# Attention and mixture-of-experts kernel: GpSimd issues only DMAs during the attention, and V tiles and expert weights go out in small portions

## The chip, the core and the metric

The kernel runs on one core of a Trainium2 chip. The metric is the device time of one execution in microseconds (us). "Before" is the kernel as it was, "the change" the edited one. A ratio is the mean time of one kernel's fast runs over that of the other's fast runs of the same rounds, so it is not quite the ratio of the medians quoted beside it. Below 1 is faster.

The engines are TensorE (PE; its weight loads PEld), VectorE (DVE), ScalarE (ACT), GpSimd (POOL) and SyncE (SP). In the traces GpSimd starts its instructions in the order of the program: the key copy at 66.57 us below starts only after a memset in front of it has waited 6.95 us. An instruction on GpSimd that waits holds up everything behind it on GpSimd, wanted or not.

## The reference, cut

```python
# attention: B=4, H=8, S=768, D=64; 8 global keys and a causal window of 96 keys
scores = scale * q @ k.T + bias;  a = softmax(where(is_global | is_local, scores, -1e9))
x = (a @ v)  ->  [3072, 512]
# top-1 mixture of 8 experts, with skipping
do = x @ w_skip > 0
e  = argmax(x @ w_gate);  g = softmax(x @ w_gate)[e]
out = x;  out[do] += g * (relu(x @ w1[e]) @ w2[e])      # w1, w2: 512x1024 and 1024x512 per expert
```

Inputs and outputs are fp32; the kernel's tiles are mostly bf16, cast by the DMAs.

## The kernel before

The attention works in 16 units: one head pair of one batch each, four units to a batch. Unit n's loop body computes the scores of unit n+2, transposes the q and k of unit n+4 and loads the q and k of unit n+8. Batch b can start its values only when the "global scores" of the batch are done; these need the first keys of all four of its head pairs, copied into the tile `kg`. After the attention, rows are gathered from DRAM by expert, go through the experts, and are scattered to the output.

```python
def load_v(b):                               # GpSimd, all of it
    vb = v_pool.tile([128, T, H, D1], BF16)
    for t in range(T):                       # T = 6
        nc.gpsimd.dma_start(out=vb[:, t, :, 0:D], in_=v_r[b, t])
    nc.gpsimd.memset(vb[:, :, :, D:D1], 1.0) # waits until the six loads have landed

def keys_global(n):                          # two small copies
    nc.gpsimd.tensor_copy(out=kg[...], in_=kts[n][...])

def load_vg(b):                              # a 128x512 product and a 128x8 copy
    nc.gpsimd.tensor_tensor(out=vg[:, b, :, 0:D], ...)
    nc.gpsimd.tensor_copy(out=vg[:, b, :, D], in_=head_m)

load_qk(0); load_qk(1); load_qk(2); load_qk(3); load_v(0)
for n in range(4):
    transposes(n, 1); transposes(n, 0); keys_global(n)
    ...                                      # scores of units 0 and 1
    load_qk(4 + n)
    if n == 1: load_vg(0)
load_v(1)
for b in range(1, B): load_vg(b)
for n in range(16):
    if hp == 0: global_scores(b)
    scores(n + 2, 0); values(n, 0); scores(n + 2, 1)
    transposes(n + 4, 1); keys_global(n + 4)
    ...; scores(n + 2, 2); values(n, 1); transposes(n + 4, 0)
    load_qk(n + 8)
    if n in (2, 5): load_v(2 if n == 2 else 3)
    if n == 8:                               # ten DMAs of 1 MB (as bf16)
        for e in range(5): load_weights(e, wearly)
    ...                                      # gating of batch b-1
# then 16 gathers, the weights of experts 5 to 7 among them, experts, 40 scatters: DMAs from GpSimd
```

In the built program every GpSimd DMA waits for the completion of the eighth GpSimd DMA before it: at most eight are in flight. The trace of the kernel before fits: its 12th, 13th and 14th GpSimd DMAs (9.77, 10.95 and 12.13 us) wait for a q, a k and a q load, which are the 4th, 5th and 6th. I call this the line of eight.

The softmax here doesn't subtract the row's maximum and nothing guards it: scores larger than these inputs give would overflow.

Of the kernel before, what the change touches and what calls it, by code (L numbers as in the profile page):

```python
# [9 lines left out]
BF16 = mybir.dt.bfloat16  # L10
I32 = mybir.dt.int32
AX = mybir.AxisListType
ALU = mybir.AluOpType
# [4 lines left out]
def kernel(  # L18
# [13 lines left out]
    nc = tc.nc  # L32
    B, H, S, D = q.shape
    NG = int(n_global)
    NL = int(n_local)
    T = S // 128
    N = B * S
    NT = N // 128
    DM = H * D
    HP = H // 2  # L40
    E, F = moe_w1.shape[0], moe_w1.shape[2]
    DC = DM // 128
    FC = F // 128
# [7 lines left out]
    D1 = D + 1  # L51
    KG = 128 // H
    NV = 5
    RSPACE = 4096
    EARLY = 5
# [5 lines left out]
    wearly = ctx.enter_context(tc.tile_pool(name="wearly", bufs=1))  # L61
# [4 lines left out]
    acon = attn.enter_context(tc.tile_pool(name="acon", bufs=1))  # L66
# [9 lines left out]
    v_r = v.rearrange("b h (t p) d -> b t p h d", p=128)  # L76
    w1_r = moe_w1.rearrange("e (c p) f -> e p c f", p=128)
    w2_r = moe_w2.rearrange("e (c p j) d -> e p c (j d)", p=128, j=2)

    units = [(b, hp) for b in range(B) for hp in range(HP)]  # L80
    raws, qts, kts, g_sbs, a_sbs, vbs = {}, {}, {}, {}, {}, {}

    def load_qk(n):
        b, hp = units[n]
        qr = raw_pool.tile([P, 2, R * D], BF16, tag="qr", name="qr")
        kr = raw_pool.tile([P, 2, R * D], BF16, tag="kr", name="kr")
        nc.gpsimd.dma_start(out=kr[:, :, :], in_=k_r[b, :, 2 * hp:2 * hp + 2, :])
        nc.gpsimd.dma_start(out=qr[:, :, :], in_=q_r[b, :, 2 * hp:2 * hp + 2, :])
        raws[n] = (qr, kr)

    def load_v(b, ones=True):
        vb = v_pool.tile([128, T, H, D1], BF16, tag="vb", name="vb")
        for t in range(T):
            nc.gpsimd.dma_start(out=vb[:, t, :, 0:D], in_=v_r[b, t])  # L94
        nc.gpsimd.memset(vb[:, :, :, D:D1], 1.0)
        vbs[b] = vb

    w1_sb, w2_sb = {}, {}

    def load_weights(e, pool):  # L100
        w1_sb[e] = pool.tile([128, DC, F], BF16, name=f"w1_{e}")
        w2_sb[e] = pool.tile([128, FC // 2, 2 * DM], BF16, name=f"w2_{e}")
        nc.gpsimd.dma_start(out=w1_sb[e][:, :, :], in_=w1_r[e])
        nc.gpsimd.dma_start(out=w2_sb[e][:, :, :], in_=w2_r[e])

    manual = tc.manual_schedule()
    manual.__enter__()
# [2 lines left out]
    nc.gpsimd.iota(row128_i[:, :], pattern=[[1, 128]], base=0, channel_multiplier=0)  # L110
    part_i = setup.tile([128, 1], I32)
    nc.gpsimd.iota(part_i[:, :], pattern=[[0, 1]], base=0, channel_multiplier=1)
    load_qk(0)
    load_qk(1)
    load_qk(2)
    load_qk(3)
    load_v(0)
    colid_i = setup.tile([128, NCOL], I32)
    nc.gpsimd.iota(colid_i[:, :], pattern=[[RSPACE // 128, E], [1, CAP // 128]], base=0,
                   channel_multiplier=0)  # L120
# [9 lines left out]
    for h in range(H):  # L130
        nc.sync.dma_start(out=vg_f[h * KG:(h + 1) * KG, :, :],
                          in_=v[:, h, 0:KG, :].rearrange("b k d -> k b d"))
    wg_f = acon.tile([128, DC, E + 1], FP32)
    for dc in range(DC):
# [3 lines left out]
    part_f = setup.tile([128, 1], FP32)  # L138
# [3 lines left out]
                            scalar2=None, op0=ALU.is_equal)  # L142
    kg = []
    for s in range(2):
# [6 lines left out]
                            scalar2=None, op0=ALU.subtract)  # L151
    nc.vector.tensor_scalar(out=rel[:, 128:W], in0=row128_i[:, 0:NL], scalar1=part_f[:, 0:1],
                            scalar2=128.0, op0=ALU.subtract, op1=ALU.add)
    far = acon.tile([128, W], FP32)
    for bound, op in ((0.0, ALU.is_lt), (float(NL), ALU.is_ge)):
        nc.vector.tensor_scalar(out=far[:, :], in0=rel[:, :], scalar1=bound, scalar2=1.0e6,
                                op0=op, op1=ALU.mult)
        nc.vector.tensor_tensor(out=rel[:, :], in0=rel[:, :], in1=far[:, :], op=ALU.add)
    mask8 = acon.tile([128, H, 2, W], BF16)
    for h in range(H):  # L160
        nc.scalar.activation(out=mask8[:, h, :, :],
                             in_=rel[:, :].unsqueeze(1).to_broadcast([128, 2, W]),
# [5 lines left out]
                                   op=ALU.arith_shift_right)  # L168
    gkey_i = acon.tile([128, 1], I32)
    nc.vector.tensor_single_scalar(out=gkey_i[:, :], in_=part_i[:, :], scalar=KG - 1,  # L170
                                   op=ALU.bitwise_and)
# [6 lines left out]
    head_m = acon.tile([128, H], FP32)  # L178
    nc.vector.tensor_scalar(out=head_m[:, :], in0=row128_i[:, 0:H], scalar1=ghead[:, 0:1],
                            scalar2=None, op0=ALU.is_equal)  # L180
    gconst = acon.tile([128, H], FP32)
    for h in range(H):
# [5 lines left out]
                            op0=ALU.mult)  # L188
    grel = acon.tile([128, 128], FP32)
    nc.vector.tensor_scalar(out=grel[:, :], in0=row128_i[:, :], scalar1=gk[:, 0:1], scalar2=None,  # L190
                            op0=ALU.subtract)
# [2 lines left out]
    nc.vector.tensor_single_scalar(out=grel[:, :], in_=grel[:, :], scalar=float(NL), op=ALU.is_ge)  # L194
    m0g = acon.tile([128, 128], BF16)
    nc.vector.tensor_tensor(out=m0g[:, :], in0=gw1[:, :], in1=grel[:, :], op=ALU.add)
    vg = acon.tile([128, B, H, D1], BF16)

    def load_vg(b):
        nc.gpsimd.tensor_tensor(  # L200
            out=vg[:, b, :, 0:D],
            in0=vg_f[:, b, :].unsqueeze(1).to_broadcast([128, H, D]),
            in1=head_m[:, :].unsqueeze(2).to_broadcast([128, H, D]), op=ALU.mult)
        nc.gpsimd.tensor_copy(out=vg[:, b, :, D], in_=head_m[:, :])

    ones_bf = setup.tile([128, 128], BF16)
    nc.vector.memset(ones_bf[:, :], 1.0)
# [2 lines left out]
                            op0=ALU.is_ge)  # L210
# [10 lines left out]
    def late_constants():  # L221
        nc.vector.tensor_copy(out=wg[:, :, :], in_=wg_f[:, :, :])
        nc.vector.tensor_copy(out=eorder[:, :], in_=eorder_i[:, 0, :])
        nc.vector.tensor_copy(out=run[:, :], in_=eorder_i[:, 1, :])
        nc.vector.tensor_copy(out=val_k[:, :, 1], in_=tt_i[:, :])
        nc.vector.tensor_copy(out=val_k[:, :, 0], in_=part_f[:, 0:1].to_broadcast([128, NT]))
        nc.vector.memset(slots[:, :, :], 0.0)
# [3 lines left out]
    def transposes(n, which):  # L231
        b, hp = units[n]
        raw = raws[n][which]
        ps = ps_ms.tile([128, R, P], BF16, tag="ms", name="tr")
        for r in range(R):
            for hh in range(2):
                nc.tensor.transpose(out=ps[hh * D:(hh + 1) * D, r, :],
                                    in_=raw[:, hh, r * D:(r + 1) * D], identity=ident[0:P, 0:P])
        if which == 0:
            qt = t_pool.tile([128, R, P], BF16, tag="qt", name="qt")  # L240
            nc.vector.tensor_copy(out=qt[:, :, :].bitcast(I32), in_=ps[:, :, :].bitcast(I32))  # L241
            qts[n] = qt
        else:
            kt = t_pool.tile([128, S], BF16, tag="kt", name="kt")
            nc.scalar.activation(out=kt[:, :].rearrange("a (p r) -> a p r", r=R),  # L245
                                 in_=ps[:, :, :].rearrange("a r p -> a p r"),
                                 func=ACT.Copy)
            kts[n] = kt

    def keys_global(n):  # L250
        b, hp = units[n]
        for hh in range(2):
            h = 2 * hp + hh
            nc.gpsimd.tensor_copy(out=kg[b % 2][hh * D:(hh + 1) * D, hp, h * KG:(h + 1) * KG],  # L254
                                  in_=kts[n][hh * D:(hh + 1) * D, 0:KG])

    def global_scores(b):
        g_sb = att_pool.tile([128, S], BF16, tag="g_sb", name="g_sb")
# [83 lines left out]
    def x_out(b):  # L342
        nc.sync.dma_start(
            out=x_dram[b * S:(b + 1) * S, :].rearrange("(t p) d -> p t d", p=128),
            in_=xbs[b][:, :, :])
# [116 lines left out]



    for n in range(4):
        transposes(n, 1)
        transposes(n, 0)
        keys_global(n)
        if n < 2:
            for g in range(3):  # L470
                scores(n, g)
        load_qk(4 + n)
        if n == 1:
            load_vg(0)
    late_constants()
    load_v(1)
    for b in range(1, B):
        load_vg(b)
    for n in range(NU):
        b, hp = units[n]  # L480
        if hp == 0:
            global_scores(b)
        m, j = n + 4, n + 2
        if j < NU:
            scores(j, 0)
        values(n, 0)
        if j < NU:
            scores(j, 1)
        if m < NU:
            transposes(m, 1)  # L490
            keys_global(m)
        if b > 0 and hp < 3:
            logits(b - 1, hp)
        if j < NU:
            scores(j, 2)
        values(n, 1)
        if m < NU:
            transposes(m, 0)
        if m + 4 < NU:
            load_qk(m + 4)  # L500
        if n in (2, 5):
            load_v(2 if n == 2 else 3)
        if n == 8:
            for e in range(EARLY):
                load_weights(e, wearly)
        if hp == HP - 1:
            x_out(b)
        if b > 0 and hp == 2:
            gate(b - 1)
        if b > 0 and hp == 3:  # L510
            gate_rest(b - 1)
            place((b - 1) * T, T, colid_i, gat_pool, ps_ms, "ms")
# [9 lines left out]
    wlate = ctx.enter_context(tc.tile_pool(name="wlate", bufs=1, reuse_waits="tile"))  # L522
# [76 lines left out]
    def experts(group, first):  # L599
        rows, src, gate_ = slot_rows()  # L600
        for e in range(E):
            gather(e, src)
            if first and e % 2 == 1 and EARLY + e // 2 < E:
                load_weights(EARLY + e // 2, wlate)
        xt = expert_in(0)
        for e in range(E):
            nxt = expert_in(e + 1) if e + 1 < E else None
            expert(e, xt, rows, gate_, group)
            if first:
                for t in range(3 * e, 3 * e + 3):  # L610
                    skip_out(t, group)
            xt = nxt

    experts("first", True)
    manual.__exit__(None, None, None)

# [5 lines left out]
                                   op=ALU.bitwise_and)  # L622
# [5 lines left out]
                                   op=ALU.arith_shift_right)  # L628
# [3 lines left out]
    with tc.For_i(1, n_rounds, 1):  # L632
        nc.vector.tensor_single_scalar(out=colid[:, :], in_=colid[:, :], scalar=CAP // 128,
                                       op=ALU.add)
# [38 lines left out]
```

## Time and profile before

| what | value |
|---|---|
| median time | 260.75 us (3 runs, 259.92 to 261.82) |
| profiled span | 260.2 us (of a run of 262.22 us) |
| global scores of batch 0 / 1 / 2 / 3 done | 30.7 / 68.8 / 97.9 / 126.6 us |
| last attention output done, first gather | 141.3, 157.2 us |
| last scatter issued | 248.8 us |

The page's slices show the span in 40 parts of 6.5 us; a digit is the busy share in tenths, PEclk the granted TensorE clock in tenths.

```profile
PE   1561698200696849854972511799992599994000
...
PEclk9999999655599558965797755589999599999655
DMA  5993991599449992999999998999999344434420
```

TensorE is nearly empty in the fourth slice and in slices 8 to 10 (46 to 65 us). The GpSimd timeline says why. Its columns are start, duration, engine, line, operation, output<-input, shape, count, and in brackets the idle time before it with what ended that.

```profile
12.13 0.87 POOL L94 DMA_DIRECT2D vb<-in_v_dram  x1 [0.31 <-DMA qr<-in_q_dram]
21.41 0.31 POOL L95 MEMSET vb<- 128x48 bf16 x1 [8.40 <-DMA vb<-in_v_dram]
...
30.00 5.29 POOL L94 DMA_DIRECT2D vb<-in_v_dram  x6
42.01 0.32 POOL L95 MEMSET vb<- 128x48 bf16 x1 [6.71 <-DMA vb<-in_v_dram]
...
57.43 1.82 POOL L94 DMA_DIRECT2D vb<-in_v_dram  x2 [1.68 <-DMA kr<-in_k_dram]
66.20 0.31 POOL L95 MEMSET vb<- 128x48 bf16 x1 [6.95 <-DMA vb<-in_v_dram]
66.57 0.44 POOL L254 COPY kg<-kt 64x16 bf16<-64x16 bf16 x2
```

Three of the four memsets stand 6.7 to 8.4 us behind V loads. The key copy at 66.57 comes right after the third one, although it had nothing to do with V. The list of waits adds up who paid (total us, number of times, longest):

```profile
POOL vb L95 <- DMA vb<-in_v_dram: 26.9, 4, 8.4
...
PE gp L262 <- POOL kg L254: 29.9, 8, 15.5
...
PE tr L237 <- DMA kr<-in_k_dram: 4.9, 1, 4.9
```

GpSimd's own waits were 26.9 us; TensorE's wait for the key copies behind them was 29.9 us. A table of stages, cut at the times above, gives for each stretch its length, then busy us and instruction count of PE, PEld, DVE, ACT and POOL, the mean granted clock, the DMA share (in this view it can exceed 1) and GB/s:

```profile
30.70:68.80 38.10, 17.15 (x298) 11.48 (x298) 14.89 (x33) 13.84 (x22) 21.77 (x36) 0.73 1.20 108
68.80:97.90 29.10, 22.01 (x360) 15.97 (x361) 19.47 (x59) 17.07 (x26) 12.24 (x23) 0.73 1.01 120
97.90:126.60 28.70, 21.25 (x359) 15.52 (x361) 19.45 (x59) 17.01 (x26) 8.94 (x18) 0.74 0.90 166
126.60:141.30 14.70, 9.73 (x192) 7.93 (x191) 11.50 (x40) 8.37 (x13) 0.00 (x0) 0.96 1.12 225
141.30:157.20 15.90, 4.80 (x67) 4.18 (x67) 9.37 (x42) 2.29 (x3) 0.00 (x0) 0.61 1.11 227
157.20:260.20 103.00, 65.24 (x449) 43.59 (x449) 17.69 (x29) 19.03 (x32) 60.58 (x62) 0.81 0.64 149
```

The first row is batch 0 until the global scores of batch 1: 38.1 us for 17 us of TensorE work. The next two are batches 1 and 2. The fifth ends with the gather rows ready; the sixth is the experts.

### The profile page before, as it was taken

Reading aid. Unit: us, or ns where it says so; the run is one execution under the profiler, and the core shown is the slowest. Engines: PE = TensorE matmul, PEld = TensorE weight load, DVE = VectorE, ACT = ScalarE, POOL = GpSimd, SP = SyncE. Lnnn points to the kernel's source line nnn. Section 1 sums busy time; section 2 is a strip of 40 time slices with the busy share of each in tenths; the row PEclk is TensorE's granted clock in tenths of the full one; section 3 lists DMA queues with packets and bytes.
Section 4 is the critical chain, followed back from the end, with each engine's and each line's share of the span. In section 5 each row is a group of like instructions: output and inputs, shape, how many; then the busy total and the mean of one; then the engine's idle time right before and its main releaser. Section 6 shows DMA issues by size and latency. Waiting matters only on the chain.

```text
span 260.2 us, 4730 instructions
## 1 busy us (share of the span) xinstructions
PE 152.4 (59%) x1877; PEld 106.7 (41%) x1877; DVE 104.2 (40%) x311; ACT 91.1 (35%) x144; POOL 123.5 (47%) x183
## 2 busy tenths in 40 slices
PE   1561698200696849854972511799992599994000
PEld 1450376000375627643662500557770277762000
DVE  7440079400268764887389380212200432323000
ACT  5860389000396508933670300023330033330000
POOL 8806945971348323611000006836261777777730
PEclk9999999655599558965797755589999599999655
DMA  5993991599449992999999998999999344434420
GB/s 84 177 127 55 154 153 8 104 202 117 62 66 138 51 216 29 199 202 210 229 229 211 229 231 179 161 238 223 226 202 244 118 133 148 136 99 117 118 52 1
DMA packets 50520, 38.24 MB, mean 147 GB/s; under 512 B 30276, under 2 KB 39492, under 8 KB 50496
## 3 DMA queue, kind: packets, MB, share of 16 engines
q0 software_dynamic: 45568, 34.62, 84.6%
q1 hardware_dynamic: 4928, 3.30, 4.9%
q8 instruction: 16, 0.26, 0.4%
q14 instruction: 8, 0.07, 0.1%
HBM read 54.68 MB, written 13.63 MB: 263 GB/s over the span
## 4 chain that ended last, share of the span: by engine, by line
DMA 35%; PE 21%; POOL 14%; DVE 10%; ACT 8%; issue 7%; POOLq 0%; ACTq 0%; DVEq 0%
DMA vb<-in_v_dram 9%; PE yps L586 7%; DMA x_rows<-xb 6%; PE hps L579 5%; DMA xg<-x_rows,src 5%; DMA w<-in_moe_w_dram 5%; DMA out_dram<-y,rows 5%; DMA kr<-in_k_dram 3%; DMA qr<-in_q_dram 3%; ACT a L287 3%; PE gp L262 3%; ACT a L295 2%; DVE xb L332 2%; POOL xg L547 2%; ACT xts L362 2%
## 5 line engine op out<-in xcount | busy, mean ns | idle before, releaser
L582 ACT ACTIVATE ht<-hps 128x512 bf16<-128x512 f32 x32 | 19.0, 597 | 66.0 <-PE hps L579 66.0
L547 POOL DMA_INDIRECT xg<-x_rows,src x16 | 15.7, 980 | 51.7 <-DMA x_rows<-xb 38.1
L301 DVE TENSOR_TENSOR a<-a,mask 128x896 bf16<-128x896 bf16 (+1 forms) x48 | 29.2, 612 | 22.3 <-ACT a L287 12.1
L586 PE MATMUL yps<-w,ht 128*128 128x512 bf16 x128 | 30.8, 394 | 7.9 <-DVE y L591 7.9
L591 DVE SCALAR_TENSOR_TENSOR y<-yps,gate,xg 128x512 f32<-128x512 f32 x16 | 11.9, 750 | 55.4 <-PE yps L586 28.5
L287 ACT ACTIVATE a<-sc 128x896 bf16<-128x896 f32 x32 | 28.9, 923 | 9.0 <-PE sc L282 8.2
L579 PE MATMUL hps<-xt,w 128*128 128x256 bf16 x256 | 31.8, 287 | 0.0
L556 POOL DMA_INDIRECT out_dram<-xb,skip_k x24 | 24.1, 1004 | 13.6 <-DMA w<-in_moe_w_dram 6.8
L262 PE MATMUL gp<-qt,kg 128*128 128x384 bf16 x32 | 11.9, 513 | 29.9 <-POOL kg L254 29.9
L579 PEld LDWEIGHTS <-w 128*128 128x128 bf16 x256 | 26.1, 103 | 4.2
L94 POOL DMA_DIRECT2D vb<-in_v_dram x24 | 21.2, 904 | 2.7 <-DMA kr<-in_k_dram 2.0
L586 PEld LDWEIGHTS <-ht 128*128 128x128 bf16 x128 | 12.8, 100 | 22.5 <-issue 9.9
L265 ACT ACTIVATE g_sb<-gp,gbias 128x384 bf16<-128x384 f32 x8 | 4.6, 581 | 48.1 <-PE gp L262 48.1
L282 PE MATMUL sc<-qt,kt 64*128 64x224 bf16 x192 | 19.8, 296 | 2.8 <-DVE qt L241 1.3
L319 PE MATMUL av<-vb,a 128*128 128x65 bf16 x192 | 19.1, 207 | 0.0
L262 PEld LDWEIGHTS <-kg 128*128 128x128 bf16 x32 | 4.0, 135 | 35.5 <-POOL kg L254 32.4
L332 DVE TENSOR_TENSOR xb<-av,rc 128x384 bf16<-128x384 f32 x32 | 17.8, 558 | 1.1
L326 PE MATMUL av<-vb,a 128*96 128x65 bf16 x160 | 18.3, 219 | 0.0
L594 POOL DMA_INDIRECT out_dram<-y,rows x16 | 15.9, 995 | 4.9 <-issue 3.7
L319 PEld LDWEIGHTS <-a 128*128 128x128 bf16 x192 | 17.0, 117 | 0.0
L326 PEld LDWEIGHTS <-a 128*96 128x96 bf16 x160 | 15.6, 138 | 0.0
L254 POOL COPY kg<-kt 64x16 bf16<-64x16 bf16 x32 | 6.7, 210 | 17.6 <-ACT kt L245 16.4
(115 smaller groups left out, 246.6 us busy)
## 6 DMA issues: line engine op xcount, KB each, us to landing
w<-in_moe_w_dram POOLq DMA_DIRECT2D x16, 1024.0 KB, 22.4
kr<-in_k_dram POOLq DMA_DIRECT2D x16, 192.0 KB, 5.2
qr<-in_q_dram POOLq DMA_DIRECT2D x16, 192.0 KB, 5.4
vb<-in_v_dram POOLq DMA_DIRECT2D x24, 128.0 KB, 6.7
x_rows<-xb SPq DMA_DIRECT2D x4, 768.0 KB, 11.4
out_dram<-xb,skip_k POOLq DMA_INDIRECT x24, 2.6
xg<-x_rows,src POOLq DMA_INDIRECT x16, 12.6
out_dram<-y,rows POOLq DMA_INDIRECT x16, 2.7
```

Source lines behind the costliest of these rows:

```text
L94: nc.gpsimd.dma_start(out=vb[:, t, :, 0:D], in_=v_r[b, t])
L262: nc.tensor.matmul(out=gp[:, :, :], lhsT=kg[b % 2][:, hp, :], rhs=qts[b * HP + hp][:, :, u * (P // 2):(u + 1) * (P // 2)], start=(hp == 0) ...
L282: nc.tensor.matmul(out=sc[:, hh, kk, 0:R * wp].rearrange("a (r p) -> a r p", r=R), lhsT=kt[rows, t * 128:(t + 1) * 128], rhs=qt[rows, :, t ...
L287: nc.scalar.activation(out=a[:, :, :].rearrange("a h (k p r) -> a h k p r", k=2, r=R), in_=sc[:, :, :, 0:W].rearrange("a h k (r p) -> a h ...
L301: nc.vector.tensor_tensor(out=a[:, :, 0:wid], in0=a[:, :, 0:wid], in1=m[:, :, 0:wid], op=ALU.mult)
L319: nc.tensor.matmul(out=av[:, jj, hh, :], lhsT=a_sbs[n, t // 2][:, hh, (t % 2) * W:(t % 2) * W + 128], rhs=vb[:, t, h, :], start=False, sto ...
L326: nc.tensor.matmul(out=av[0:NL, jj, hh, :], lhsT=a_sbs[n, p // 2][:, hh, c:c + NL], rhs=vb[:, p, h, :], start=False, stop=(jj == 2 and hh ...
L332: nc.vector.tensor_tensor(out=xb[:, 3 * u:3 * u + 3, 2 * hp * D:(2 * hp + 2) * D].rearrange("p j (h d) -> p j h d", h=2), in0=av[:, :, :, ...
L547: nc.gpsimd.indirect_dma_start(out=xg[e][:, c, :], out_offset=None, in_=x_dram[:, :], in_offset=bass.IndirectOffsetOnAxis(ap=src[:, 2 * e ...
L556: put(nc.gpsimd.indirect_dma_start(out=out[:, :], out_offset=bass.IndirectOffsetOnAxis(ap=skip_k[:, t:t + 1], axis=0), in_=xbs[t // T][:, ...
L579: nc.tensor.matmul(out=hps[:, j, :], lhsT=w1_sb[e][:, dc, c2 * 256 + j:(c2 + 1) * 256:2], rhs=xt[:, dc, :], start=(dc == 0), stop=(dc == D ...
L586: nc.tensor.matmul(out=yps[:, :], lhsT=ht[:, f // 2, f % 2, c * 128:(c + 1) * 128], rhs=w2_sb[e][:, f // 2, (f % 2) * DM:(f % 2 + 1) * DM] ...
```

## The change: its intent, and the diff

GpSimd is to hold nothing but DMA issues during the attention, so that no wait of a load stands before work that computes. The memset, key copies and vg products go to VectorE. V tiles go out three per unit and the early weight halves one per unit from unit 1 on, so that the DMA queues are filled evenly.

```diff
-    def load_v(b, ones=True):
+    def make_v(b):
         vb = v_pool.tile([128, T, H, D1], BF16, tag="vb", name="vb")
-        for t in range(T):
-            nc.gpsimd.dma_start(out=vb[:, t, :, 0:D], in_=v_r[b, t])
-        nc.gpsimd.memset(vb[:, :, :, D:D1], 1.0)
+        nc.vector.memset(vb[:, :, :, D:D1], 1.0)
         vbs[b] = vb
+    def load_v(b, t):
+        nc.gpsimd.dma_start(out=vbs[b][:, t, :, 0:D], in_=v_r[b, t])
...  load_vg: both instructions from nc.gpsimd to nc.vector
...  keys_global: two nc.gpsimd.tensor_copy become one nc.vector product with a 0/1 mask of the halves
...  start: load_v(0, 0), load_v(0, 1) before load_qk(2), load_v(0, 2) before load_qk(3)
+    extra = [V tiles of batches 1, 2, 3 in order]
+    halves = {1: 1, 2: 1, 3: 1, 4: 1, 5: 1, 6: 1, 7: 1, 8: 1, 9: 1, 10: 1}
...  in the loop over units:
         if m + 4 < NU:
             load_qk(m + 4)
-        if n in (2, 5):
-            load_v(2 if n == 2 else 3)
-        if n == 8:
-            for e in range(EARLY):
-                load_weights(e, wearly)
+        if n in (0, 2, 4):
+            make_v(1 + n // 2)
+            load_vg(1 + n // 2)
+        for kind in range(3):
+            if extra:
+                _, vb_, t = extra.pop(0)
+                load_v(vb_, t)
+        for _ in range(halves.get(n, 0)):
+            load_half(wq.pop(0), wearly)
```

More of the change, by code (lines that the diff above doesn't have):

```diff
@@ L89, in load_qk, with load_half @@
         raws[n] = (qr, kr)
-    def load_v(b, ones=True):
+    def make_v(b):
         vb = v_pool.tile([128, T, H, D1], BF16, tag="vb", name="vb")
-        for t in range(T):
-            nc.gpsimd.dma_start(out=vb[:, t, :, 0:D], in_=v_r[b, t])
-        nc.gpsimd.memset(vb[:, :, :, D:D1], 1.0)
+        nc.vector.memset(vb[:, :, :, D:D1], 1.0)
         vbs[b] = vb
+    def load_v(b, t):
+        nc.gpsimd.dma_start(out=vbs[b][:, t, :, 0:D], in_=v_r[b, t])
     w1_sb, w2_sb = {}, {}
-    def load_weights(e, pool):
-        w1_sb[e] = pool.tile([128, DC, F], BF16, name=f"w1_{e}")
-        w2_sb[e] = pool.tile([128, FC // 2, 2 * DM], BF16, name=f"w2_{e}")
-        nc.gpsimd.dma_start(out=w1_sb[e][:, :, :], in_=w1_r[e])
-        nc.gpsimd.dma_start(out=w2_sb[e][:, :, :], in_=w2_r[e])
+    def load_half(i, pool):
+        e = i // 2
+        if i % 2 == 0:
+            w1_sb[e] = pool.tile([128, DC, F], BF16, name=f"w1_{e}")
+            nc.gpsimd.dma_start(out=w1_sb[e][:, :, :], in_=w1_r[e])
+        else:
+            w2_sb[e] = pool.tile([128, FC // 2, 2 * DM], BF16, name=f"w2_{e}")
+            nc.gpsimd.dma_start(out=w2_sb[e][:, :, :], in_=w2_r[e])
     manual = tc.manual_schedule()
@@ L112 @@
     nc.gpsimd.iota(part_i[:, :], pattern=[[0, 1]], base=0, channel_multiplier=1)
+    make_v(0)
     load_qk(0)
     load_qk(1)
+    load_v(0, 0)
+    load_v(0, 1)
     load_qk(2)
+    load_v(0, 2)
     load_qk(3)
-    load_v(0)
+    for t in range(3, T):
+        load_v(0, t)
     colid_i = setup.tile([128, NCOL], I32)
@@ L196 @@
     nc.vector.tensor_tensor(out=m0g[:, :], in0=gw1[:, :], in1=grel[:, :], op=ALU.add)
+    half_m = acon.tile([128, 2], BF16)
+    nc.vector.tensor_scalar(out=half_m[:, 1:2], in0=part_f[:, :], scalar1=float(D), scalar2=None,
+                            op0=ALU.is_ge)
+    nc.vector.tensor_scalar(out=half_m[:, 0:1], in0=part_f[:, :], scalar1=float(D), scalar2=None,
+                            op0=ALU.is_lt)
     vg = acon.tile([128, B, H, D1], BF16)
     def load_vg(b):
-        nc.gpsimd.tensor_tensor(
+        nc.vector.tensor_tensor(
             out=vg[:, b, :, 0:D],
@@ L203, in load_vg @@
             in1=head_m[:, :].unsqueeze(2).to_broadcast([128, H, D]), op=ALU.mult)
-        nc.gpsimd.tensor_copy(out=vg[:, b, :, D], in_=head_m[:, :])
+        nc.vector.tensor_copy(out=vg[:, b, :, D], in_=head_m[:, :])
     ones_bf = setup.tile([128, 128], BF16)
@@ L251, in keys_global @@
         b, hp = units[n]
-        for hh in range(2):
-            h = 2 * hp + hh
-            nc.gpsimd.tensor_copy(out=kg[b % 2][hh * D:(hh + 1) * D, hp, h * KG:(h + 1) * KG],
-                                  in_=kts[n][hh * D:(hh + 1) * D, 0:KG])
+        nc.vector.tensor_tensor(
+            out=kg[b % 2][:, hp, 2 * hp * KG:2 * (hp + 1) * KG].rearrange("p (h k) -> p h k", h=2),
+            in0=kts[n][:, 0:KG].unsqueeze(1).to_broadcast([128, 2, KG]),
+            in1=half_m[:, :].unsqueeze(2).to_broadcast([128, 2, KG]), op=ALU.mult)
     def global_scores(b):
@@ L461, in place @@
         nc.vector.tensor_tensor(out=slots[:, :, :], in0=slots[:, :, :], in1=sp[:, :, :], op=ALU.add)
+    extra = [("v", 1, t) for t in range(T)]
+    wq = list(range(2 * EARLY))
+    for b in (2, 3):
+        extra += [("v", b, t) for t in range(T)]
+    halves = {1: 1, 2: 1, 3: 1, 4: 1, 5: 1, 6: 1, 7: 1, 8: 1, 9: 1, 10: 1}
     for n in range(4):
@@ L472 @@
         load_qk(4 + n)
-        if n == 1:
-            load_vg(0)
+    load_vg(0)
     late_constants()
-    load_v(1)
-    for b in range(1, B):
-        load_vg(b)
     for n in range(NU):
@@ L603, in experts @@
             if first and e % 2 == 1 and EARLY + e // 2 < E:
-                load_weights(EARLY + e // 2, wlate)
+                load_half(2 * (EARLY + e // 2), wlate)
+                load_half(2 * (EARLY + e // 2) + 1, wlate)
         xt = expert_in(0)
```

## The prediction

> **What bounds the kernel now.** By the chain of waits and the GpSimd timeline, three stretches.
>
> 1. Start, 12 to 30.6 us. GpSimd issues the last V tile at 12.1 us, then sits 8.4 us before the ones-memset of that V buffer, until its DMAs land (21.4). The global-key copies queue behind it on the in-order engine; the global scores are only complete at 30.6, although the last transposes ended at 18.4.
> 2. Attention, 31 to 141 us. Batch 0's four units take 14 us. GpSimd repeats the pattern: memset waiting 6.7 us (35 to 42), 4.5 us of vg products, issues, then memset waiting 7 us more (59 to 66). TensorE is idle in 51.6 to 67.1 (15.5 us charged to the global-key copy) and, but for three matmuls, from 45. Batches 1 and 2 take 28 us each, batch 3 some 17, limited by the VectorE/ScalarE/TensorE chain (each 60 to 75% busy).
> 3. 141 to 260 us. Gathers start at 157.2. The x_rows write (15 us, shared with the late early-weight traffic) ends the wait, but VectorE delivers the gather rows only at 155.9, so the write hides about 1 us. Then gathers, 6.3 MB of late weights and 40 scatters at 1.3 us each: GpSimd issue and DMA bound, 103 us.
>
> **What the change does.** No GpSimd instruction in the attention waits for a V transfer in front of compute work. VectorE gets 16 key products (about 0.2 us), 4 vg products (estimate 0.7 us, from the 128x384 product's 0.56) with casts, 4 memsets: 6 us in all, perhaps 4 on the path, as VectorE is nearly limiting. GpSimd's elementwise work no longer overlaps VectorE: during the vg products the mask product took 1.45 us instead of 0.62. The Trainium skill (GPSIMD Engine Reference, Specifications) says the two share SBUF interfaces when VectorE has two SBUF inputs; this trace agrees.
>
> **Size.**
> - Start: the loop begins near 21.5 instead of 30.6: -9 us.
> - Batch 0 to 1: global scores of batch 1 finish near 40 instead of 68.8; of this -9 is the start, so -20 net of about 2.5 us of VectorE work.
> - Rest of attention: +2 us of VectorE work.
> - Given back: the DMA queue. Measured rates: V 155 GB/s, q/k about 175, weights 213. One unit's q/k+V+weight half is 2.25+2.55+4.9 = 9.7 us (estimate) against 7 us of compute. q/k loads fall behind near units 9 to 11 and stall transposes: +4 us (0 to 10).
> - x_rows no longer shares with weights: -0.7 only, since the row computation ends at the same time.
> - Gathers to end: unchanged, 103 us. Early weights land near 115 instead of 153, but nothing waits for them.
>
> Attention ends near 118 instead of 141.3. Predicted time: 237 us, range 226 to 248. Chances: faster 0.96, same 0.03, slower 0.01.
>
> **What would show it.** GpSimd timeline: no memset, no copies, only DMA issues until the first gather, which comes near 133. TensorE's 15.5 us gap before the global scores gone; those of batch 0 done near 21.5, of batch 1 near 40. A TensorE wait for k/q DMAs of a few us in batch 2 or at its end would confirm the give-back. Weight landings within 50 to 120. Time from last attention output to first gather still about 15 us, first gather to end still about 103.
>
> **What would make it wrong.** Only eight GpSimd DMAs are in flight; weight halves in that line could delay q/k or V far more than 4 us (towards 250). Denser TensorE work may be granted a lower clock (it alternates 1.0 and 0.5 now), lengthening batches and experts. If the final stage was itself slowed by the weight backlog, 225 is possible.

## More of the kernel before

The gap in `vb` that the memset fills lies between the bytes that the DMAs write, so the dependency tracking takes the two as overlapping and orders them as written (this is read from the program; the trace shows the wait).

For k tiles TensorE waited once, at the very first load.

## The result, and the profile after

The change ran in 243.35 us (median of 4 runs, 242.59 to 243.99) against 260.34 us before; ratio 0.938, 95% interval 0.930 to 0.946. Executions over 1.5% slower than the fastest of the same kernel are left out of the means. Of the four runs before, 261.82 us is 1.7% above the fastest, which counts as slow. The profiled span fell from 260.2 to 242.2 us (runs of 262.22 and 243.99 us).

The slices of the change, now 6.05 us each:

```profile
PE   1579895995494847768544038699943999992000
...
PEclk9999998897569575559857556999995799998555
DMA  5999999999999999999630039999994355343310
```

The holes in TensorE's row in the first third are gone, and the DMA row is full until 115 us; TensorE has new thin slices, the 4s at 73 to 79 and 85 to 91 us (slices 13 and 15). Slice 11 is a 4 too, but there it waits 3.41 us for VectorE's gating work, as it also did before (up to 4.2 us). The same table of stages as before:

```profile
21.50:40.70 19.20, 15.27 (x299) 11.21 (x300) 15.57 (x43) 13.87 (x22) 13.92 (x18) 1.00 1.38 161
40.70:69.80 29.10, 22.09 (x359) 16.07 (x361) 21.06 (x67) 17.16 (x26) 12.15 (x17) 0.73 1.39 212
69.80:108.10 38.30, 25.43 (x359) 18.55 (x361) 20.35 (x63) 17.33 (x26) 8.31 (x12) 0.63 1.29 208
108.10:123.20 15.10, 11.13 (x191) 9.13 (x191) 11.51 (x40) 8.53 (x13) 0.00 (x0) 0.84 0.76 156
123.20:138.80 15.60, 4.97 (x67) 4.35 (x67) 9.45 (x43) 2.29 (x3) 0.00 (x0) 0.61 0.15 52
138.80:242.20 103.40, 65.10 (x449) 43.40 (x449) 17.93 (x29) 19.10 (x32) 60.55 (x62) 0.80 0.61 143
```

| stage | before | change | difference |
|---|---|---|---|
| start to global scores of batch 0 | 30.7 | 21.5 | -9.2 |
| batch 0, to global scores of batch 1 | 38.1 | 19.2 | -18.9 |
| batch 1 | 29.1 | 29.1 | 0.0 |
| batch 2 | 28.7 | 38.3 | +9.6 |
| batch 3 | 14.7 | 15.1 | +0.4 |
| last output to first gather | 15.9 | 15.6 | -0.3 |
| gathers, experts, end | 103.0 | 103.4 | +0.4 |
| sum | 260.2 | 242.2 | -18.0 |

In the list of waits, the one for key copies on GpSimd is gone, a short one for VectorE is left, and the one for k has grown:

```profile
PE tr L251 <- DMA kr<-in_k_dram: 13.3, 4, 5.1
...
PE gp L276 <- DVE qt L255: 2.9, 1, 2.9
```

GpSimd still waits for other engines: the three V loads at 28.18 us waited 3.97 us for VectorE to write the ones of their buffer, and the q load at 46.09 us waited 4.46 us for a transpose on TensorE.

Of the 28 us won in front, batch 2 gives a third back. TensorE's timeline shows where: it waits for a k tile in two of the batch's transposes.

```profile
79.73 0.85 PE L251 MATMUL tr<-ident,kr 96*64 96x96 bf16 x16 [4.26 <-DMA kr<-in_k_dram]
...
89.22 0.85 PE L251 MATMUL tr<-ident,kr 96*64 96x96 bf16 x16 [3.53 <-DMA kr<-in_k_dram]
```

The GpSimd timeline shows the lateness. These lines are from units 5 and 6:

```profile
61.67 0.78 POOL L108 DMA_DIRECT2D w<-in_moe_w_dram  x1
62.66 0.65 POOL L87 DMA_DIRECT2D kr<-in_k_dram  x1 [0.21 <-PE av L340]
67.13 0.64 POOL L88 DMA_DIRECT2D qr<-in_q_dram  x1 [3.83 <-DMA w<-in_moe_w_dram]
...
73.43 0.75 POOL L105 DMA_DIRECT2D w<-in_moe_w_dram  x1 [0.19 <-issue]
74.64 0.65 POOL L87 DMA_DIRECT2D kr<-in_k_dram  x1 [0.46 <-PE sc L296]
79.28 0.64 POOL L88 DMA_DIRECT2D qr<-in_q_dram  x1 [3.99 <-DMA w<-in_moe_w_dram]
```

The k tile issued at 62.66 is the one that TensorE starts on at 79.73, 17 us later. The q issues behind the k issues wait 3.8 to 4.0 us each for a weight half: the line of eight is full. The Trainium skill (DMA: Bandwidth & Descriptors, section "Two DMAs through the same engine are not ordered") says that within one queue of one DMA engine descriptors start in order. That a small load behind a large one therefore waits for it is my inference, and this trace agrees: the weight half issued at 61.67 is the eighth DMA before the q issue of 79.28, which its landing released, and the k tile issued 1 us after that half landed at 79.7. Over all k tiles the median time from issue to landing rose from 5.2 to 7.8 us, the longest from 8.3 to 17.0 us.

### The profile page after: what moved, and what is told of

Its sections match the earlier page's. It is cut to its first block, busy times and chain, and to the rows that moved or that the text cites. A ratio compares the mean times of both kernels' runs of the same rounds, so it can differ in the third digit from the quotient of the medians.

```text
span 242.2 us, 4714 instructions
## 1 busy us (share of the span) xinstructions
PE 155.8 (64%) x1877; PEld 110.8 (46%) x1877; DVE 109.1 (45%) x341; ACT 91.8 (38%) x144; POOL 111.0 (46%) x139
## 5 line engine op out<-in xcount | busy, mean ns | idle before, releaser
L315 DVE TENSOR_TENSOR a<-a,mask 128x896 bf16<-128x896 bf16 (+1 forms) x48 | 28.2, 588 | 21.8 <-ACT a L301 11.7
L599 PE MATMUL hps<-xt,w 128*128 128x256 bf16 x256 | 31.2, 283 | 0.0
L97 POOL DMA_DIRECT2D vb<-in_v_dram x24 | 21.5, 906 | 11.3 <-DMA vb<-in_v_dram 4.0
L333 PE MATMUL av<-vb,a 128*128 128x65 bf16 x192 | 20.7, 215 | 0.0
L251 PE MATMUL tr<-ident,kr 96*64 96x96 bf16 x256 | 11.4, 251 | 13.3 <-DMA kr<-in_k_dram 13.3
L340 PE MATMUL av<-vb,a 128*96 128x65 bf16 x160 | 19.7, 229 | 0.0
L88 POOL DMA_DIRECT2D qr<-in_q_dram x16 | 10.4, 650 | 19.2 <-DMA w<-in_moe_w_dram 11.7
L333 PEld LDWEIGHTS <-a 128*128 128x128 bf16 x192 | 18.6, 125 | 0.0
L614 POOL DMA_INDIRECT out_dram<-y,rows x16 | 15.9, 994 | 4.9 <-issue 3.7
L340 PEld LDWEIGHTS <-a 128*96 128x96 bf16 x160 | 17.1, 147 | 0.0
L251 PEld LDWEIGHTS <-kr 96*64 96x64 bf16 x256 | 8.8, 140 | 17.1 <-DMA kr<-in_k_dram 14.0
L259 ACT ACTIVATE kt<-tr 128x768 bf16<-128x768 bf16 x16 | 13.0, 810 | 8.5 <-PE tr L251 8.5
```

The costliest lines, as they stand in the source:

```text
L97: nc.gpsimd.dma_start(out=vbs[b][:, t, :, 0:D], in_=v_r[b, t])
L251: nc.tensor.transpose(out=ps[hh * D:(hh + 1) * D, r, :], in_=raw[:, hh, r * D:(r + 1) * D], identity=ident[0:P, 0:P])
L315: nc.vector.tensor_tensor(out=a[:, :, 0:wid], in0=a[:, :, 0:wid], in1=m[:, :, 0:wid], op=ALU.mult)
L333: nc.tensor.matmul(out=av[:, jj, hh, :], lhsT=a_sbs[n, t // 2][:, hh, (t % 2) * W:(t % 2) * W + 128], rhs=vb[:, t, h, :], start=False, sto ...
L340: nc.tensor.matmul(out=av[0:NL, jj, hh, :], lhsT=a_sbs[n, p // 2][:, hh, c:c + NL], rhs=vb[:, p, h, :], start=False, stop=(jj == 2 and hh ...
L599: nc.tensor.matmul(out=hps[:, j, :], lhsT=w1_sb[e][:, dc, c2 * 256 + j:(c2 + 1) * 256:2], rhs=xt[:, dc, :], start=(dc == 0), stop=(dc == D ...
```

## The experiments

Theory Q: the early weight halves, placed in the line ahead of q and k, cost batch 2 its 9.6 us. Theory V, its rival: the work added to VectorE, or a lower granted clock (0.63 in batch 2 against 0.74), lengthened it. A second pair concerns the gain. Theory M: nearly all of it is the memset no longer waiting. Theory E: the elementwise work had to leave GpSimd. Every run gave the reference's result, within its tolerance. Call 1 (first four runs) and call 3 (last four) had the kernel before at 260.79 and 260.17 us. Call 2 fell on a chip where it took 270.46 us, so its runs are compared by ratio.

### Weights back at unit 8

```diff
-    halves = {1: 1, 2: 1, 3: 1, 4: 1, 5: 1, 6: 1, 7: 1, 8: 1, 9: 1, 10: 1}
+    halves = {8: 10}
```

> The changed kernel with one part undone: all ten early weight halves issued at head pair 8, as before the change. Theory Q (the weight halves stand in the DMA line ahead of the q/k loads and cost batch 2 its 9.3 us): the two k waits of 4.3 and 3.5 us vanish, batch 2 takes 26 to 27 us again instead of 35.6, time 233 to 236 us. Theory V (batch 2 is longer because of VectorE's added work or a lower granted clock): batch 2 stays near 35 us, time 242 to 244 us. Both: gathers to end unchanged at 103 us, as long as the weights land before the gathers.

Measured: 234.73 us, ratio 0.901 (0.897 to 0.905). The waits of TensorE for k, and the batch 2 row of its stage table:

```profile
PE tr L251 <- DMA kr<-in_k_dram: 5.2, 1, 5.2
```

```profile
69.40:98.30 28.90, 21.45 (x360) 15.65 (x361) 20.07 (x63) 17.01 (x26) 1.49 (x2) 0.74 1.12 221
```

The one wait left is the very first load of the kernel. Batch 2 takes 28.9 us with 20.1 us of VectorE work, against 28.7 us with 19.5 us before. So the added VectorE work costs nothing measurable there, and theory Q holds. (The expectation cut batch 2 differently, 35.6 us where the table has 38.3; its 26 to 27 us was not reached, but the drop of 9.4 us is the 9.3 that it named.) The clock is back at 0.74 too: its drop went with the waiting. The Trainium skill (TensorE: Matmul & The Clock Gate, section "What's actually happening") says the default state is throttled and activity releases it. These two rows agree, but TensorE's busy share over a stage does not settle the clock: batch 3 before and batch 2 of the change were both 66% busy (9.73 of 14.70 and 25.43 of 38.30 us) and were granted 0.96 and 0.63. That the clock explains the 1.8 us by which 9.6 exceeds the two waits of 7.8 is argued, not shown. The repeat of the change speaks against a large part: batch 1 took 29.1 us there too, at a clock of 0.79 instead of 0.73, and batch 2 took 37.9 us at 0.68, 9.1 us more than with the weights at unit 8, of which its k waits explain 7.0.

### Weights twice as dense

```diff
-    halves = {1: 1, 2: 1, 3: 1, 4: 1, 5: 1, 6: 1, 7: 1, 8: 1, 9: 1, 10: 1}
+    halves = {1: 2, 2: 2, 3: 2, 4: 2, 5: 2}
```

> The changed kernel with two weight halves per head pair at pairs 1 to 5 instead of one at pairs 1 to 10. Theory Q: one half takes 4.9 us in the line (estimate from 1 MB at 213 GB/s), so the k loads of units 13 and 14 land some 20 to 24 us later, TensorE waits for them that much longer, and the time rises to 260 to 268 us. Theory V: the order of weights does not matter, 242 to 244 us.

Measured: 267.66 us, ratio 1.027 (1.022 to 1.032): slower than the kernel before.

```profile
PE tr L251 <- DMA kr<-in_k_dram: 34.5, 6, 8.2
```

The k waits grow to 34.5 us (of which about 5 are the first load), and 24 us of time follow. The same bytes, placed earlier in the same line, turn a gain of 6% into a loss of 3%.

### The kernel before with one line moved

```diff
         vb = v_pool.tile([128, T, H, D1], BF16, tag="vb", name="vb")
+        nc.gpsimd.memset(vb[:, :, :, D:D1], 1.0)
         for t in range(T):
             nc.gpsimd.dma_start(out=vb[:, t, :, 0:D], in_=v_r[b, t])
-        nc.gpsimd.memset(vb[:, :, :, D:D1], 1.0)
```

> The kernel before with one line moved: GpSimd writes the ones of a V buffer before its six loads instead of after. All else stays on GpSimd, V in blocks of six, weights at pair 8. Theory M (the memset's wait for the V loads is nearly the whole cost of the old schedule): global scores of batch 0 done near 22 us, of batch 1 near 45 us (GpSimd still does three vg products and six issues in between), batch 2 without k waits, time 234 to 242 us. Theory E (the elementwise work itself must leave GpSimd): the global scores of batch 1 stay later than 55 us, time above 248 us.

Measured: 240.26 us, ratio 0.921 (0.917 to 0.925). This one line alone beats the whole change (ratio 0.938, 0.930 to 0.946).

```profile
PE gp L262 <- POOL kg L254: 7.6, 3, 5.8
```

TensorE's wait for the key copies falls from 29.9 to 7.6 us. Global scores of batch 0 and 1 are done at 23.3 and 47.1 us (change: 21.5 and 40.7), and there is no k wait in the attention, as the weights stayed at unit 8. Theory M is right for the larger part. Batch 1 still starts 6.4 us later than in the change, which differs in several ways; what the elementwise work on GpSimd costs is measured further down, under "V in blocks again".

### The change with the copies and products back on GpSimd

```diff
-        nc.vector.tensor_tensor(out=kg[...], in0=kts[n][...], in1=half_m[...], op=ALU.mult)
+        for hh in range(2):
+            nc.gpsimd.tensor_copy(out=kg[...], in_=kts[n][...])
...  load_vg: both instructions from nc.vector to nc.gpsimd
```

> The changed kernel with the key copies and vg products back on GpSimd (memset stays on VectorE, V and weights as changed). Theory M: the copies alone cost little, the time stays within 3 us of 243; VectorE's 5 us of extra work was mostly hidden, so nothing is gained either. Theory E: the copies wait for ScalarE in front of the DMA issues and the products delay them, so the time rises above 248 us.

Measured: 253.75 us median; two of the four runs were slow, and the two fast ones are 250.04 and 252.91 us. I expected about 243 us on theory M; that was wrong. The wait of TensorE, and GpSimd around the last key copy of batch 2:

```profile
PE gp L276 <- POOL kg L268: 16.2, 4, 8.0
```

```profile
83.38 0.63 POOL L88 DMA_DIRECT2D qr<-in_q_dram  x1 [5.29 <-DMA w<-in_moe_w_dram]
84.75 0.77 POOL L108 DMA_DIRECT2D w<-in_moe_w_dram  x1 [0.73 <-DMA kr<-in_k_dram]
85.57 0.42 POOL L268 COPY kg<-kt 64x16 bf16<-64x16 bf16 x2
```

The copy at 85.57 stands behind a q load that waited 5.29 us for a weight half, and a weight issue; TensorE's longest wait, 8.0 us, ends with it. The copies also hold GpSimd up, as theory E said: they waited 19.4 us in all for ScalarE to deliver `kt`, 3.39 us of it at 29.34 us in front of a k issue. My reading is that copies on GpSimd cost more the fuller the line of eight is. The next edit was to test it.

### The same with the weights at unit 8

```diff
     # the edit above, and
-    halves = {1: 1, 2: 1, 3: 1, 4: 1, 5: 1, 6: 1, 7: 1, 8: 1, 9: 1, 10: 1}
+    halves = {8: 10}
```

> V spread, weights at pair 8, but the key copies and vg products on GpSimd. Theory L (copies on GpSimd hurt in proportion to the time GpSimd is blocked by the line of eight transfers; the weight halves were most of that): the waits of the global scores for the GpSimd copies fall from 16.2 us to 4 to 9 us, time 237 to 241 us, near the 240.3 us of the one-line version. Theory E (copies on GpSimd are bad whatever the line holds): 246 us or more, as with early weights.

Measured: 250.30 us median beside 270.46 us before, but three of four runs, the profiled one included, were slow. The one fast run, 246.21 us, is 0.91 of the kernel before. In the profiled run TensorE waited 6.0 us for the copies (16.2 with early weights), inside the 4 to 9 us of theory L. Theory L's 237 to 241 us are ratios of 0.91 to 0.92 on the first chip, theory E's 246 us is 0.94, so 0.91 fits theory L. With one fast run, and the waits read from a slow one, this is only an indication.

### V in blocks again

```diff
-    load_qk(0); load_qk(1); load_v(0, 0); load_v(0, 1); load_qk(2); load_v(0, 2); load_qk(3); ...
+    load_qk(0); load_qk(1); load_qk(2); load_qk(3); six load_v(0, t)
+    make_v(1); load_vg(1); six load_v(1, t)        # ahead of the loop over units
...  in the loop: make_v, load_vg and six load_v at units 2 and 5, no spread tiles, weights at unit 8
```

> Key products, vg products and ones-memset on VectorE as in the change; V in blocks of six tiles where the kernel before had them, first q/k loads before V, and all ten weight halves at pair 8. Only the spreading of V is missing against the run with the weights at pair 8 (234.7 us). If spreading V is worth nothing once no compute work stands behind the loads on GpSimd: 233 to 236 us, no k waits in the attention. If the spreading itself is needed: k waits of several us in batch 1, 239 us or more.

Measured on the slower chip: 241.76 us (one of four runs slow), ratio 0.890 (0.880 to 0.900). No k waits in the attention. The chips differed, so I repeated it beside the change and the version with weights at unit 8:

> The changed kernel itself, as the control on this chip for the three runs below. Batch 2 again shows two k waits of 3 to 5 us; ratio to the kernel before 0.93 to 0.945.

> The changed kernel with all early weight halves at head pair 8, repeated beside the control. Theory Q: 8 to 10 us below the control, ratio to the kernel before 0.895 to 0.907.

> As the run before it with V in blocks of six. The first look was on another chip, where the kernel before was slower too, and its attention ended 3 us earlier than that of the spread version on the first chip. If that is the order of the loads: 2 to 4 us below the spread version here. If it was the chip or its granted clock: within 1 us of it.

| kernel, 6 runs each | median us | ratio to before, 95% |
|---|---|---|
| the change | 243.13 | 0.937 (0.931 to 0.942) |
| weights at unit 8 | 234.62 | 0.903 (0.898 to 0.907) |
| weights at unit 8, V in blocks | 230.70 | 0.888 (0.883 to 0.892) |

One of the six runs of the change was slow; the median of its fast runs is 243.03 us. The control repeated its two k waits, 3.81 and 3.17 us. V in blocks is 3.9 us faster than V spread, within what the "order of the loads" reading expected. But the spans' 3.5 us difference has no single place: start -0.7, batch 0 -0.6, batch 1 -0.4, batch 2 -1.0, batch 3 +0.7, to the first gather -0.4, the rest -1.1 us. The edit also moves one vg product out of batch 0 and shifts the granted-clock stretches. Which of these it is stays open. What is shown is that spreading V, with the changed order of the first loads, was not worth anything once the weights were back at unit 8: with VectorE holding the memset, little was left on GpSimd that six V issues in a row could hold up.

This version also settles what the elementwise work costs, for it has the schedule of the one-line version and differs from it only in that memset, copies and products run on VectorE, the products partly at another moment. The ratio goes from 0.921 to 0.888, some 9 us (different chips, so by the ratios). By the spans, 7.8 of 8.8 us are won before batch 1, which starts at 39.3 instead of 47.1 us. So theory E is right for a smaller part.

### Looking for more: scatters of skipped rows during the attention

The last stage issues 40 scatters at 1.3 us each, 24 of them for rows that skip the experts. Those of batches 0 to 2 could go out during the attention, when GpSimd is idle.

```diff
+            for t in range((b - 1) * T, b * T):      # after the gating of batch b-1
+                skip_out(t, "first")
...  experts: only the skip_out of batch 3 is left
```

> The run with weights at pair 8, and the 18 skip scatters of batches 0 to 2 issued on GpSimd during the attention instead of among the expert outputs. If the last stage is bound by GpSimd's 1.3 us per scatter (40 of them, 52 us), it becomes bound by TensorE (8 experts of 7.4 us plus an 8 us wait for y): last scatter about 8 us earlier, time 224 to 230 us. If the stage is bound by the DMA line or by TensorE already: no gain, 234 us.

A second version also issues the two halves of expert 5 ahead of the gathers:

```diff
+            load_half(2 * EARLY, wlate); load_half(2 * EARLY + 1, wlate)   # before the gathers
-            if first and e % 2 == 1 and EARLY + e // 2 < E:               # later experts' weights
+            if first and e in (3, 5):
```

> As the run with early skip scatters, and the two weight halves of expert 5 issued before the gathers instead of between them. If GpSimd's waits for the line of eight (about 10 us among the gathers) delay the first expert outputs and cause TensorE's 7.6 us wait for y: the gathers end 5 to 10 us earlier, that wait shrinks, time 4 to 8 us less than the run with early skip scatters. If the halves are still landing when the gathers start, the first gather lands later and the gain is lost.

Measured on the slower chip: ratios 0.889 (0.882 to 0.896) and 0.882 (0.875 to 0.889). The first gather slipped to 138.7 and 141.5 us, since scatters wait in the line of eight behind weight halves, and the weights in turn wait behind the first scatters (in the first version they start at 72.9 instead of 59.4 us). In the second, the halves ahead of the gathers delayed the first gathered rows until 153 us, 11.7 us after their gather, against 2.8 us in the first. Their base, weights at unit 8 with V spread, did not run on this chip, so what the early scatters gained or lost over it is not measured. I then put the scatters behind the weights, on the version with V in blocks:

```diff
+        if n in (8, 12):                     # after the ten halves of unit 8
+            for t in range((n // 4 - 2) * T, (n // 4 - 1) * T):
+                skip_out(t, "first")
+    for t in range(2 * T, 3 * T):            # after the loop over units
+        skip_out(t, "first")
...  experts: only the skip_out of batch 3 is left
```

> V in blocks, all early weights at pair 8, and the 18 skip scatters of batches 0 to 2 issued behind the weights, before the gathers, instead of among the expert outputs. In the earlier try they stood partly before the weights and held the first gather back from 129 to 139 us. If the line of eight lets them pass between the last weight (near 110 us) and the first gather (near 127 us): first gather within 3 us of the V-in-blocks run, last scatter 3 to 8 us earlier after it, time 3 to 8 us less. If they still block the gathers: no gain or a loss.

Measured beside it: 231.18 us (two of six runs slow), ratio 0.888 (0.882 to 0.893): no gain, the second of the two outcomes. The GpSimd timeline:

```profile
93.66 0.98 POOL L482 DMA_INDIRECT out_dram<-xb,skip_k  x1 [4.99 <-DMA w<-in_moe_w_dram]
...
122.93 0.98 POOL L482 DMA_INDIRECT out_dram<-xb,skip_k  x1 [5.23 <-DMA w<-in_moe_w_dram]
...
137.22 1.01 POOL L582 DMA_INDIRECT xg<-x_rows,src  x1 [0.30 <-issue]
```

The early scatters wait about 5 us each for weight halves until 123 us, so the rest run until 137 us and the first gather goes out at 137.2 instead of 127.0 us. The last scatter was issued at 218.5 us against 218.2: the 10 us saved at the end were spent in front. These three runs missed my numbers. The version with weights at unit 8 and V in blocks, 230.7 us, beats both the kernel before and the change. Whether it is the best stays open: the second scatter version had 239.02 us and 0.882 beside its 241.76 us and 0.890, with overlapping intervals, and the two edits were not tried together.

## Why the prediction was right, and where it was off

The predicted direction and range held: 243.35 us lies in 226 to 248, 6 us above the 237 us that was called most likely.

- "Start: the loop begins near 21.5 instead of 30.6: -9 us." Measured 21.5 and -9.2.
- "Global scores of batch 1 finish near 40": measured 40.7, and -18.9 us net of the start where I said -20.
- "+2 us of VectorE work" in the rest, besides the 2.5 us inside batch 0: too high. Batch 1 took 29.1 us both times while VectorE's busy time rose from 19.5 to 21.1 us. Batch 2 without k waits took 28.9 us against 28.7. The work filled gaps in which VectorE waited anyway. Inside batch 0 its price was not measured alone.
- "q/k loads fall behind near units 9 to 11 and stall transposes: +4 us (0 to 10)." The mechanism and the place were right (units 9 and 10), the size was the main error: +9.6 us, of which 7.8 are two k waits. Taking the weights out of the line removed 9.4 us of it. The estimate summed transfer times; it left out that each issue also waits for the eighth transfer before it, which shows as 3.8 to 4.0 us in front of the q issues, though the prediction's last paragraph named this very risk. It also set 9.7 us a unit against 7 us of compute, while the four units of batch 0 took 19.2 us, 4.8 us each, so in units 1 to 3 the queue fell behind by about 4.9 instead of 2.7 us a unit (estimate from these numbers). How much of the excess is each of these and how much the lower clock, the runs do not separate.
- "x_rows ... -0.7 only" and "gathers to end: unchanged, 103 us": measured -0.3 and +0.4. Early weights ending sooner bought nothing, as said.

What the prediction did not see is the split of the gain. It treated the change as one piece. The runs give it step by step, as ratios to the kernel before: the one moved line 0.921, then the elementwise work on VectorE 0.888, then V spread 0.903, then the weights early 0.937, which is the change. A single reordered line gives 20.5 of the 260.8 us, the other work moved to VectorE some 9 us more, and two of the change's parts work against them: early weights cost 8.5 us, V in portions with the changed order of the first loads 3.9 us (both by the medians of call 3).

## What to carry to other kernels

Look at what an in-order engine that issues DMAs also has to do between the issues, and at each of these instructions' waits; write constants into a buffer before its loads, not after. Filling a DMA queue evenly was no gain in itself here: a transfer that is needed late must not enter the line ahead of one that is needed soon, even if the queue then idles for a while. When a change bundles several moves, run the smallest of them alone; it may carry more than the whole.

## What the Trainium skill lacked or had wrong

- "DMA: Bandwidth & Descriptors" has nothing on a limit of transfers in flight as a program may set it. In this program it is eight per GpSimd queue, and waits for it show as up to 5.6 us in front of the next issue when 1 MB halves fill the line, be that issue a 192 KB load (3.8 to 5.3 us), a gather (4.0), a scatter (5.2) or the next half (5.6).
- The same page gives its measured SWDGE rates for copies of up to 425 GB/s at 16 MB. Casting loads (fp32 to bf16) here moved about 213 GB/s of written bytes for 1 MB halves, so twice that, some 426 GB/s, of bytes read (estimate), and about 155 GB/s written for V tiles, whose rows are 64 elements; the page has no row for casting loads.
- The Specifications of "GPSIMD Engine Reference" give the contention with VectorE for SBUF no size. Here a VectorE mask product took 1.45 us instead of 0.62 us beside a GpSimd product. The reverse showed as well: a vg product on GpSimd took 1.45 instead of 1.04 us when a mask product on VectorE had started just before it (30.02 and 30.09 us in the one-line version). On VectorE the vg product took 0.69 to 0.77 us, so GpSimd took 1.4 to 1.5 times as long undisturbed, where section 3.1 of the page measured 1.96 times for an fp32 add of another size; the shapes differ, so this does not contradict it.
- No page says how much chips differ: the kernel before took 260.2 us, and 270.5 us on another chip (whether it is the chip or its state then is open). The V-in-blocks version, run on both, reached the first gather after 127.0 and 125.9 us, but took 102.5 and 113.8 us from there on. Kernels are to be compared on one chip.
